# A fused adaLN block with attention and MLP: padding the last MLP tile, a new order of the tail, first loads on two rings, and reused buffers whose new writers are not ordered among themselves

## The chip, the cores and the metric

The kernel runs on one core of a Trainium2 chip. The metric is the device time of one execution, in microseconds (us), as the median of several. "PE" is the matmul engine and "PEld" its weight loads, "DVE" the vector engine, "ACT" the activation engine, "POOL" the general-purpose engine, and "SP" the engine that in this kernel does nothing but issue transfers. ACT and POOL issue transfers too. A "score" matmul multiplies queries by K, a "PV" matmul the result by V. hT is the normalised x of a chunk, transposed, from which the queries are made (the "first projection"). An issuing engine has a "ring", the queue that its transfers stand in.

## The reference, cut to what matters

```python
x = A_x                                    # 2048 x 640, bf16
sa, ca, ga, sb, cb, gb = split(silu(c) @ w_mod)        # 640 -> 6 x 640
h = layernorm(x) * (1 + ca) + sa
x = x + ga * attention(h, k_cache, v_cache, wq, wo)    # 32 heads of 128, 2048 keys
h = layernorm(x) * (1 + cb) + sb
x = x + gb * B(h)

def B(x):                                  # F = 1728 = 13 * 128 + 64
    h  = gelu(layernorm(x) @ w1)
    hs = concat(four column groups of h, shifted by 1, -1, 2, -2 rows) @ w2
    x1 = x + hs
    return x1 + gelu(layernorm(x1) @ w3) @ w4
```

F is not a multiple of 128: the last of the 14 tiles of W3's columns and W4's rows has 64.

## The kernel before

The kernel is written for a list scheduler. Every operation names its engine, what it reads and writes, and a priority; `Plan` puts the operations of each engine in one order and adds the semaphores. The queries are split in four chunks of 512. Attention is a long steady part; the MLP, the tail, comes at the end. Parts of the tail are named by letters: A is W1 of a chunk, B is W2 of 128 rows, C is W3 of a chunk, D is W4 of 128 rows, WO is the last output projection of attention, and I3 the layer norms of the last chunk. K0, V0, V1, V3 are the K and V of head 0, 1, 3; W_o and Wq are the weights of the output and the query projections; X1 is the x of chunk 1.

```python
class Plan:
    FIRST = {"PE": 3, "ACT": 10000, "DVE": 0, "POOL": 7, "SP": -5}   # where the branch to the fast program stands
    HINT  = {"PE": 0, "ACT": -30, "DVE": 0, "POOL": 0, "SP": -12}    # and its prefetch hint

    def op(self, eng, fn, dur, reads=(), writes=(), prio=0.0, ...):
        for t in reads:
            for d in t.writer: o.deps[d] = True
            t.readers.append(o)
        for t in writes:
            ...
            for d in t.writer:  o.deps.setdefault(d, False)   # a new writer waits for the last writer
            for d in t.readers: o.deps[d] = True              # and for the readers
            t.writer = [o]                                    # and is the writer that the next one waits for
            t.readers = []
# ... the start: K transposes, Wq, x and most V on SP; the gate weights and V0 on ACT
    dma("ACT", lambda e: e.dma_start(pre_ap, mod_src(2)), 800, (wm[1],), pre_t, -292)      # gate weights
    load_v(0, -290, "ACT", gate=(wm[1],))                                                  # V0
    load_wq(0, 1, HG, -295.985, gate=(wm[2],))                                             # Wq, heads 1 to 3, on SP
# ... two of the five slices of hT of chunk 0 are made by ACT, the others by DVE
            for k in (0, 2, 4, 1, 3):
                if k % 2:
                    P.op("ACT", lambda e, k=k: e.activation(hT_t[0][:, k, :], hslice(k, 0, 4), ACT.Identity, ...
# ... the transposes of the normalised chunk into a buffer that held other data (nT_old)
                dmaT(lambda e, i=i: e.dma_start_transpose(nT_ap[ch][:, :, i * 128:(i + 1) * 128], xn[i].ap), 160,
                     (xn[i],), (nT[ch][i],) + nT_old[ch](), prio)
# ... the tail
    TAIL = ("A0 B0 B1 A1 B2 B3 WO B4 B5 I3 A2 B6 C0 B7 D0 D1 D2 B8 D3 B9 C1 D4 A3 B10 B11 "
            "B12 D5 B13 D6 B14 D7 B15 C2 D8 D9 D10 D11 C3 D12 D13 D14 D15").split()
    WOD, CH, I3D = -100, -1000, -200
    def w4_tile(t, key):
        for hf in range(2):
            for f in range(NF):                    # NF = 14, FS = [128] * 13 + [64]
                fs = FS[f]
                P.op("PE", lambda e, ...: e.matmul(m[:, hf * 512:hf * 512 + HD], gT_ap[0:fs, f, i * 128:(i + 1) * 128],
                                                   w4_ap[f][0:fs, hf * HD:(hf + 1) * HD], start=(f == 0), stop=(f == NF - 1)), ...
```

## Time and profile before

| | us |
|---|---|
| time before, median of 3 | 1391.6 (1391.36 to 1391.62) |
| profiled span | 1391.3 |
| first score matmul | 18.11 |
| first W1 matmul (the tail begins) | 1207.44 |
| from there to the end | 183.9 (1391.3 - 1207.44) |

These are two lines of the page of the kernel before: PE's busy time with its share of the span, and the shares of the chain that ended last.

```profile
PE 1379.4 (99%) x13128; PEld 941.2 (68%) x13128; DVE 539.6 (39%) x1401; ACT 1101.5 (79%) x1143; POOL 100.9 (7%) x88
...
PE 97%; DVE 1%; DMA 1%; SPq 0%; issue 0%; ACT 0%
```

PE is busy all the time, and the chain is PE. So a change can pay only at PE: fewer or quicker matmuls, or fewer of its few waits.

The next lines are from PE's timeline before, in the tail. Columns: start, duration, engine, line of the program, operation, output from inputs, shapes, count, and in brackets the idle time before it and what ended it.

```profile
1258.56 4.28 PE L928 MATMUL f_M<-f_KV,f_OO 128*128 128x320 bf16 x28
1262.77 4.29 PE L928 MATMUL f_S<-f_KV,f_OO 128*128 128x320 bf16 x28
```

One W4 tile follows the other every 4.22 us, with 28 matmuls each. The timeline of PE's weight loader shows what is peculiar in each tile:

```profile
1260.42 1.85 PEld L928 LDWEIGHTS f_M<-f_KV,f_OO 64*128 64x128 bf16 x14 [0.26 <-issue]
1262.53 0.09 PEld L928 LDWEIGHTS f_M<-f_KV,f_OO 64*128 64x128 bf16 x1 [0.26 <-issue]
```

The loader stands still 0.26 us around each load of 64 rows (usually 0.04).

PE's timeline at the last output projection, before:

```profile
1225.74 0.71 PE L691 MATMUL f_S<-f_wo,f_OO 128*128 128x320 bf16 x4
1227.88 0.72 PE L691 MATMUL f_O<-f_wo,f_OO 128*128 128x320 bf16 x4 [1.43 <-DVE f_tmp L702]
...
1229.67 1.25 PE L691 MATMUL f_O<-f_wo,f_OO 128*128 128x320 bf16 x4 [0.54 <-DVE f_small L500]
1230.72 1.27 PE L691 MATMUL f_S<-f_wo,f_OO 128*128 128x320 bf16 x4
1231.78 2.14 PE L887 MATMUL f_M<-f_W,f_PQ 128*128 128x320 bf16 x10
```

There are two waits for DVE, 1.43 and 0.54 us, and then matmuls at half speed (1.25 us for the same group that took 0.72). The windows view gives a granted clock of 0.50 between 1230 and 1232 us.

PE's timeline at the start, before:

```profile
13.38 0.25 PE L448 MATMUL f_M<-f_s_bf,f_W 128*128 128x1 bf16 x4 [1.34 <-issue]
...
18.11 0.59 PE L734 MATMUL f_S<-f_PQ,f_KV 128*128 128x512 bf16 x2
...
49.17 0.61 PE L753 MATMUL f_O<-f_KV,f_PQ 128*128 128x129 bf16 x8 [1.94 <-DMA f_KV<-in_A_v_cache_dram]
```

A gap of 1.34 us with no releaser ("issue"), the first score matmul at 18.11, and a wait of 1.94 us for V3. PE's early branch itself is at 6.4 us (by the view of its line, L252).

### The profile page before, as it was taken

To read this page: it belongs to the slowest core of one execution; us is meant where nothing else is said; L and a number is where in the kernel's file an instruction comes from. 1 tells how busy PE (TensorE), PEld (TensorE's weight loads), DVE (VectorE), ACT (ScalarE), POOL (GpSimd) and SP (SyncE) were. 2 spreads that over 40 slices of the span, in tenths; PEclk is the share of its full clock that TensorE was granted. 3 is DMA by queue.
4 is the path that set the end of the run, shared out by engine and by line. 5 is a ranking of instruction groups with operands and counts; after the bars stand their busy time and mean duration, and the time that the engine had idled before them with its cause. 6 is when DMAs were issued, how large, how long until landed. Compare 5 with 4: busy or idle time off the path is not lost.

```text
span 1391.3 us, 29861 instructions
## 1 busy us (share of the span) xinstructions
PE 1379.4 (99%) x13128; PEld 941.2 (68%) x13128; DVE 539.6 (39%) x1401; ACT 1101.5 (79%) x1143; POOL 100.9 (7%) x88
## 2 busy tenths in 40 slices
PE   9999999999999999999999999999999999999999
PEld 6667767777777777777777776777776766645554
DVE  5453232333233322333233323332333245987553
ACT  5888888888888898888888888888888888732222
POOL 0000000000000000000000000000333248200000
PEclk9999999999999999999999999999999999999999
DMA  9651623161214221241205122612254102531210
GB/s 220 130 115 31 117 78 83 36 107 35 46 36 84 58 46 36 48 92 30 54 17 98 31 45 36 107 36 46 55 91 114 17 16 48 120 53 24 53 43 25
DMA packets 259179, 88.90 MB, mean 64 GB/s; under 512 B 236705, under 2 KB 257762, under 8 KB 259042
## 3 DMA queue, kind: packets, MB, share of 16 engines
q1 hardware_dynamic: 255762, 84.59, 30.7%
q10 hardware_dynamic: 3280, 2.33, 0.7%
q8 instruction: 105, 1.72, 0.5%
q14 instruction: 32, 0.26, 0.1%
HBM read 43.48 MB, written 2.62 MB: 33 GB/s over the span
## 4 chain that ended last, share of the span: by engine, by line
PE 97%; DVE 1%; DMA 1%; SPq 0%; issue 0%; ACT 0%
PE f_O L753 33%; PE f_S L734 31%; PE f_M L666 10%; PE f_M L691 10%; PE f_M L928 3%; PE f_S L914 2%; PE f_O L914 2%; PE f_S L928 2%; PE f_S L887 1%; PE f_S L864 1%; PE f_O L864 1%; PE f_M L887 1%; DMA f_W<-in_w_mod_dram 0%; DMA f_KV<-in_A_v_cache_dram 0%; SPq L573 0%; PE f_M L610 0%
## 5 line engine op out<-in xcount | busy, mean ns | idle before, releaser
L736 ACT ACTIVATE f_PQ<-f_S 128x1024 bf16<-128x1024 f32 x1024 | 1041.0, 1023 | 148.2 <-PE f_S L734 135.1
L753 PEld LDWEIGHTS f_O<-f_KV,f_PQ 128*128 128x128 bf16 x8192 | 589.4, 98 | 233.7 <-issue 2.4
L734 PE MATMUL f_S<-f_PQ,f_KV 128*128 128x512 bf16 x2048 | 726.9, 379 | 0.2 <-ACT f_PQ L736 0.2
L753 PE MATMUL f_O<-f_KV,f_PQ 128*128 128x129 bf16 x8192 | 713.0, 220 | 2.7 <-DMA f_KV<-in_A_v_cache_dram 1.9
L699 DVE TENSOR_TENSOR f_y<-f_M,f_y 128x320 f32<-128x320 f32 x192 | 94.3, 491 | 536.3 <-PE f_M L691 536.3
L691 PE MATMUL f_M<-f_wo,f_OO 128*128 128x320 bf16 x992 | 272.9, 299 | 0.0
L734 PEld LDWEIGHTS f_S<-f_PQ,f_KV 128*128 128x128 bf16 x2048 | 196.7, 97 | 30.5 <-ACT f_PQ L736 1.2
L666 PE MATMUL f_M<-f_hT,f_wq 128*128 128x512 bf16 x640 | 177.3, 381 | 1.1 <-DVE f_hT L568 0.6
L691 PEld LDWEIGHTS f_M<-f_wo,f_OO 128*128 128x128 bf16 x992 | 96.1, 98 | 28.5
L762 DVE TENSOR_TENSOR f_OO<-f_O,f_rl 128x256 bf16<-128x256 f32 x256 | 108.4, 423 | 8.1
L669 DVE CAST f_PQ<-f_M 128x512 bf16<-128x512 f32 x128 | 88.5, 691 | 56.9 <-PE f_M L666 56.8
L520 POOL TENSOR_TENSOR f_y<-f_y,f_mod 128x640 f32<-128x640 f32 x32 | 49.6, 1560 | 820.1 <-DVE f_y L699 819.9
L666 PEld LDWEIGHTS f_M<-f_hT,f_wq 128*128 128x128 bf16 x640 | 62.2, 98 | 65.9 <-DVE f_hT L575 1.5
L760 DVE RECIPROCAL f_rl<-f_O 128x2 f32<-128x2 f32 x256 | 43.4, 169 | 32.1 <-PE f_O L753 27.9
L928 PE MATMUL f_M<-f_KV,f_OO 128*128 128x320 bf16 (+1 forms) x308 | 47.1, 300 | 0.0
L917 ACT ACTIVATE f_OO<-f_O 128x512 bf16<-128x512 f32 (+1 forms) x28 | 16.6, 596 | 38.5 <-PE f_O L914 38.5
L526 ACT ACTIVATE f_xn<-f_y,f_small 128x640 bf16<-128x640 f32 x10 | 9.1, 915 | 41.6 <-DVE f_small L505 41.6
L928 PEld LDWEIGHTS f_M<-f_KV,f_OO 128*128 128x128 bf16 (+1 forms) x308 | 28.6, 97 | 18.7 <-issue 7.0
L697 DVE COPY f_y<-f_M 128x320 f32<-128x320 f32 x32 | 15.7, 490 | 63.5 <-PE f_M L691 63.5
L481 DVE BATCH_NORM_STATS2 f_small<-f_y 128x6 f32<-128x320 f32 x64 | 29.6, 480 | 2.0 <-POOL f_y L520 2.0
L917 ACT ACTIVATE f_OO<-f_S 128x512 bf16<-128x512 f32 (+1 forms) x28 | 16.7, 595 | 13.1 <-PE f_S L914 13.1
L942 DVE TENSOR_TENSOR f_y<-f_M,f_y 128x640 f32<-128x640 f32 x10 | 8.2, 825 | 43.2 <-PE f_M L928 43.2
(134 smaller groups left out, 513.9 us busy)
## 6 DMA issues: line engine op xcount, KB each, us to landing
f_KV<-in_A_v_cache_dram SPq DMA_DIRECT2D x31, 512.0 KB, 4.8
f_wo<-in_A_wo_dram SPq DMA_DIRECT2D x8, 640.0 KB, 4.4
f_xin<-in_A_x_dram SPq DMA_DIRECT2D x15, 320.0 KB, 4.6
f_wq<-in_A_wq_dram SPq DMA_DIRECT2D x7, 640.0 KB, 4.6
f_W<-in_w_mod_dram SPq DMA_DIRECT2D x3, 800.0 KB, 4.9
out_dram<-f_xin SPq DMA_DIRECT2D x15, 160.0 KB, 1.8
f_KV<-in_B_w_dram SPq DMA_DIRECT2D x5, 432.0 KB, 3.3
f_KV<-in_A_k_cache_dram SPq DMA_TRANSPOSE x128, 2.7
```

The source lines that it names most:

```text
L520: P.op(eng, lambda e: e.tensor_tensor(out=out, in0=a, in1=b, op=op), COST[eng][0], rd, wr, prio, lat=300 if eng == "POOL" else None)
L666: P.op("PE", lambda e, i=i, kk=kk: e.matmul(m.ap, wq_t[g % 2][:, kk, hh * 128:(hh + 1) * 128], hT_t[ch][:, kk, :], start=(i == 0), stop=(i ...
L669: P.op("DVE", lambda e: e.tensor_copy(q.ap, m.ap), 690, (m,), (q,), s * NP - 90)
L691: P.op("PE", lambda e, m=m, qt=qt, hf=hf, hh=hh: e.matmul(m[:, 0:HD], OT_ap[gs][:, qt, hh, :], wo_t[g % 2][:, hh, hf * HD:(hf + 1) * HD], ...
L699: P.op("DVE", lambda e, m=m, yt=yt: e.tensor_tensor(out=yt.ap, in0=m[:, 0:HD], in1=yt.ap, op=ALU.add), 490, (m, yt), (yt,), s * NP - 60)
L734: P.op("PE", lambda e, sp=sp, r=r, kt=kt: e.matmul(sp[:, r * QC:(r + 1) * QC], K_ap[b][:, kt * 128:(kt + 1) * 128], q.ap, start=True, stop ...
L736: x = P.op("ACT", lambda e, sp=sp, pt=pt: e.activation(pt.ap.rearrange("p k q -> p (k q)"), sp.ap, ACT.Exp, scale=SCALE), 1021, (sp,), (pt ...
L753: ins = e.matmul(o[bk][:, w * 129:w * 129 + 129], pt[:, r, qt * 128:(qt + 1) * 128], V_ap[b][:, u, 0:129], start=(u == 0 and w == 0), stop ...
L760: P.op("DVE", lambda e, ov=ov, i0=i0: e.reciprocal(rl_t[:, i0:i0 + 2].unsqueeze(2), ov[:, 0:258].rearrange("p (u d) -> p u d", u=2)[:, :, ...
L762: evac.append(P.op("DVE", lambda e, ov=ov, i0=i0, bk=bk: e.tensor_tensor(out=On_ap[gs][:, 2 * bk:2 * bk + 2, hh, :], in0=ov[:, 0:258].rear ...
L914: P.op("PE", lambda e, m=m, f=f, kk=kk, fs=fs: e.matmul(m[0:fs, :], w3_ap[:, kk, f * 128:f * 128 + fs], nT_ap[ch][:, kk, :], start=(kk == ...
L928: P.op("PE", lambda e, f=f, hf=hf, fs=fs: e.matmul(m[:, hf * 512:hf * 512 + HD], gT_ap[0:fs, f, i * 128:(i + 1) * 128], w4_ap[f][0:fs, hf ...
```

## The change

It has five parts.

1. **Padding.** The last tile of W3 and W4 gets 128 columns and rows, the added half set to zero, so that no matmul has another shape.
2. **Tail order.** The last output projection moves behind W1 of chunk 2, and the DVE work that empties its banks gets priority.
3. **Start.** The first loads are divided between SP and ACT. ACT now issues the gate weights, Wq of heads 1 to 3, X1, V0 and V1; X1 goes into a buffer that nothing uses yet at the start.
4. **Writers not ordered.** A new argument `over` makes a new writer of a reused buffer wait for the old readers and writers, but the new writers do not wait for one another.
5. **Branch.** The branch to the fast program moves to the end of the first block on PE, DVE and POOL, with its prefetch hints. The scheduler's cost constants are adjusted too.

The diff, cut to its core:

```diff
-    FIRST = {"PE": 3, "ACT": 10000, "DVE": 0, "POOL": 7, "SP": -5}
-    HINT = {"PE": 0, "ACT": -30, "DVE": 0, "POOL": 0, "SP": -12}
+    FIRST = {"PE": 100000, "ACT": 100000, "DVE": -6, "POOL": 100000, "SP": -5}
+    HINT = {"PE": -300, "ACT": -30, "DVE": -60, "POOL": -1, "SP": -12}
@@ Plan.op
+        for t in over:
+            for d in t.writer:
+                o.deps.setdefault(d, False)
+            for d in t.readers:
+                o.deps[d] = True
@@ start
+            dma("ACT", lambda e: e.dma_start(y_t[:, 4:8, :].bitcast(BF16)[:, :, 0:D], x2d[512:1024, :]...),
+                640, (), xs + held, -296.7, after=(wm_load[3], ln0[1]))
-    dma("ACT", lambda e: e.dma_start(pre_ap, mod_src(2)), 800, (wm[1],), pre_t, -292)
+    dma("ACT", lambda e: e.dma_start(pre_ap, mod_src(2)), 800, (wm[3],), pre_t, -297, after=(ln0[0],))
-    load_v(0, -290, "ACT", gate=(wm[1],))
+    load_v(0, -296.5, "ACT", after=(ln0[1],))
+        if h in (1, 2, 3):
+            load_k(h, (-294, -291, -289)[h - 1], (wm[2],), () if h < 3 else from_slot(12))
+            load_v(h, (-293, -290, -289.5)[h - 1], "ACT" if h == 1 else "SP", () if h == 1 else (wm[2],), after=(ln0[1],) if h == 1 else ())
+            return
-    load_wq(0, 1, HG, -295.985, gate=(wm[2],))
+    load_wq(0, 1, HG, -296.8, eng="ACT", after=(ln0[0],))
@@ tail
-    TAIL = ("A0 B0 B1 A1 B2 B3 WO B4 B5 I3 A2 B6 C0 B7 D0 D1 D2 B8 D3 B9 C1 D4 A3 B10 B11 "
-            "B12 D5 B13 D6 B14 D7 B15 C2 D8 D9 D10 D11 C3 D12 D13 D14 D15").split()
+    TAIL = ("A0 B0 B1 A1 B2 B3 B4 A2 WO I3 B5 B6 C0 B7 D0 D1 D2 D3 B8 C1 B9 B10 A3 D4 B11 "
+            "B12 D5 B13 D6 D7 B14 B15 C2 D8 D9 D10 D11 C3 D12 D13 D14 D15").split()
-    WOD, CH, I3D = -100, -1000, -200
+    WOD, CH, I3D = -1000, -1000, -150
-                     (xn[i],), (nT[ch][i],) + nT_old[ch](), prio)
+                     (xn[i],), (nT[ch][i],), prio, over=nT_old[ch]())
@@ the same over= for the loads of W3 and W4, gT and some memsets (cut)
+    P.op("POOL", lambda e: e.memset(w3_ap[:, :, FF:FP], 0.0), 300, (), (pad,), E + 12, over=kv(2, 3, 4))
+    P.op("DVE", lambda e: e.memset(w4_ap[NF - 1][FL:128, :], 0.0), 400, (), (pad2,), E + 12, slack=500.0, over=kv(4))
-                P.op("PE", lambda e, ...: e.matmul(m[0:fs, :], w3_ap[:, kk, f * 128:f * 128 + fs], nT_ap[ch][:, kk, :],
+                P.op("PE", lambda e, ...: e.matmul(m.ap, w3_ap[:, kk, f * 128:(f + 1) * 128], nT_ap[ch][:, kk, :],
-                P.op("PE", lambda e, ...: e.matmul(..., gT_ap[0:fs, f, i * 128:(i + 1) * 128], w4_ap[f][0:fs, hf * HD:(hf + 1) * HD],
+                P.op("PE", lambda e, ...: e.matmul(..., gT_ap[:, f, i * 128:(i + 1) * 128], w4_ap[f][:, hf * HD:(hf + 1) * HD],
```

## The prediction

> **What bounds it.** The page gives PE 99% busy, the chain of waits is 97% PE, and the PE waits sum to about 10 us. Only PE time lost between matmuls, the start, and those few waits can pay.
>
> **1. Padding the last MLP tile.** Timeline of PE: a W4 tile is 28 matmuls of 320 columns and takes 4.22 us (4.12 when W2 follows, whose 10 matmuls then take 1.47 instead of 1.36). At the W2 pitch, 0.136 us, 28 would take 3.81. Around each 64-row weight load PE's loader sits idle 0.26 us for "issue", usually about 0.04. So each change between 64-row and 128-row matmuls costs about 0.11 us, four per tile. In W3 the 64-column group takes 1.20 instead of 1.08 and its successor about 0.11 more. The Trainium skill, "TensorEngine Tiling (Array Packing)", Key Properties, says that changing the tiling mode drains the engine; the trace agrees. Padded, count and streamed columns are equal and the changes vanish: 16 x 0.41 + 4 x 0.23 = -7.5 us, all on the critical path.
>
> **2. New order of the tail.** At 1225.7 to 1229.7 the last output projection waits 1.43 + 0.54 us for DVE (f_tmp evictions queued behind layer norms); then the granted clock falls to 0.50, and 4+4+10 matmuls take 1.06, 1.06 and 1.93 us instead of 0.54, 0.54 and 1.36: 1.6 us more. The change gives these evictions priority and moves them behind W1 of chunk 2. I expect -3 us.
>
> **3. Start.** The first score matmul begins at 18.1 us. A 1.34 us "issue" gap at 12.0, inside one group of matmuls, follows PE's early branch (instruction fetch, I think; the branch now stands at the end). After it the clock drops to about 0.8 and the first projection takes 2.34 instead of 1.08 us. At 47.2 PE waits 1.94 us for V of head 3, now loaded earlier. Possible gain 4 to 5 us. Against it: on the ACT ring 800 KB of gate weights, 480 KB of Wq and 640 KB of x now stand before V of head 0. The DMA share is full from 5 to 24 us at 210 to 390 GB/s; V0 landed at 20.0 and was needed at 21.8. By bytes I estimate that it now lands near 22 to 24, so PE may wait 2 to 4 us. Net -2 us (+2 to -5).
>
> **4. Writers not ordered among themselves.** This removes DMA-after-DMA waits that do not appear among PE's waits: 0.
>
> Steady attention (60 to 1195 us) should take the same time.
>
> Sum: -7.5 - 3 - 2 = -12.5 from 1391.6: **1379 us**, range 1373 to 1387. Faster by over 2% (below 1363.8) 2%, within 2% 97.5%, slower 0.5%.
>
> **What would show it.** Right: W4 tiles 3.8 us and W3 groups all 1.08; no 0.26 us loader gaps; output projection groups 0.54 each without a clock dip; first score matmul at 15.5 to 17; no V wait at 47; 60 to 1195 unchanged within 0.5 us. Wrong: W4 tiles still above 4 us; a PE wait over 3 us for V of head 0 or 1; a new DVE wait as large in the tail.
>
> **What would make the total wrong.** Late V0 with a cold clock after it (+4); DVE backlog moving to the next W2 or W3 (+3); a branch at the end of DVE or PE that costs a fetch in the output chain (+1); a start shorter by the full 5 us (-3).

## More of the kernel before

ACT's timeline at the start, before ("ACTq" is ACT issuing a transfer; the second line is V0):

```profile
7.18 0.39 ACTq L618 DMA_DIRECT2D f_KV<-in_w_mod_dram  x1
7.61 0.54 ACTq L588 DMA_DIRECT2D f_KV<-in_A_v_cache_dram  x1
...
14.25 0.78 ACT L564 ACTIVATE f_hT<-f_O,f_small 128x512 bf16<-128x512 bf16 x1 [3.02 <-PE f_M L559]
```

V0 is the last thing that ACT issues; its own part of hT begins at 14.25.

## The result, and the profile after

The kernel after takes 1387.29 us (median of 4, 1386.33 to 1387.92); the kernel before took 1391.48 (median of 4; three of them are those of the table above). A ratio here is the mean time of one kernel's fast runs over the mean of the other's fast runs of the same rounds, so it is not quite the ratio of the medians. It is 0.9973, with a 95% interval of 0.9956 to 0.999: by the limit of 2% the two are the same, and the gain is some 4 us instead of the predicted 12.5. The time lies just above the predicted range. All outputs are right.

Where it went can be read from one cut through the two traces, at the first W1 matmul:

| us | before | after | difference | predicted |
|---|---|---|---|---|
| first score matmul | 18.11 | 23.29 | +5.2 | 15.5 to 17 |
| first W1 matmul | 1207.44 | 1213.06 | +5.6 | -2 |
| from there to the end | 183.9 | 173.2 | -10.6 | -10.5 |
| profiled span | 1391.3 | 1386.3 | -5.0 | -12.5 |

The tail gained what was predicted, -10.6 against -10.5, but the close match is in part luck: the trace of the kernel before has 1.6 us of half clock that not every execution has (see "Padding alone"), and by the timing of the version with the old start the gain is nearer 9.5 us. The start lost over half of it. PE's timeline in the tail, after:

```profile
1236.49 0.71 PE L712 MATMUL f_S<-f_wo,f_OO 128*128 128x320 bf16 x4
1237.03 0.71 PE L712 MATMUL f_O<-f_wo,f_OO 128*128 128x320 bf16 x4
...
1260.26 3.97 PE L951 MATMUL f_M<-f_KV,f_OO 128*128 128x320 bf16 x28
1264.07 3.97 PE L951 MATMUL f_S<-f_KV,f_OO 128*128 128x320 bf16 x28
```

The output projection's groups come every 0.54 us without a wait, and a W4 tile takes 3.80 us instead of 4.22. Now the start, in ACT's timeline after:

```profile
8.32 0.54 ACTq L608 DMA_DIRECT2D f_wq<-in_A_wq_dram  x1
...
10.15 0.38 ACTq L552 DMA_DIRECT2D f_y<-in_A_x_dram  x1
10.57 9.59 ACTq L605 DMA_DIRECT2D f_KV<-in_A_v_cache_dram  x2
20.20 0.78 ACT L581 ACTIVATE f_hT<-f_O,f_small 128x512 bf16<-128x512 bf16 x1 [9.85 <-issue]
```

Issuing V0 and V1 takes 9.59 us (0.56 for V0, 8.99 for V1, by the view of that line's instructions). Until 20.16 ACT can do nothing else, and its two slices of hT, begun at 14.25 in the kernel before, begin at 20.20. The brackets say "issue": ACT waited for no semaphore, it was issuing. PE's timeline after shows who pays:

```profile
21.04 1.46 PE L687 MATMUL f_M<-f_hT,f_wq 128*128 128x512 bf16 x3 [6.61 <-ACT f_hT L581]
23.29 1.03 PE L755 MATMUL f_S<-f_PQ,f_KV 128*128 128x512 bf16 x2 [0.79 <-DVE f_PQ L690]
```

After the wait the matmuls run at half speed. In the windows view of after (columns: window, its length, busy time and count of PE, PEld, DVE, ACT and POOL, then the granted PE clock; the last two, the DMA share and GB/s, are not used here):

```profile
13.00:14.00 1.00, 0.39 (x1) 0.10 (x1) 1.00 (x3) 0.00 (x0) 0.00 (x0) 1.00 0.55 119
14.00:15.00 1.00, 0.39 (x1) 0.10 (x1) 0.43 (x1) 0.00 (x0) 0.00 (x0) 0.69 1.12 287
...
16.00:20.00 4.00, 0.00 (x0) 0.00 (x0) 0.00 (x0) 0.00 (x0) 0.00 (x0) 0.50 1.20 224
20.00:24.00 4.00, 2.17 (x5) 0.52 (x6) 0.69 (x1) 1.45 (x2) 0.00 (x0) 0.50 1.35 220
24.00:28.00 4.00, 4.00 (x14) 1.96 (x13) 0.61 (x2) 2.05 (x2) 0.10 (x1) 0.50 1.35 228
28.00:32.00 4.00, 4.00 (x37) 2.53 (x36) 3.18 (x9) 3.04 (x4) 0.03 (x1) 0.99 1.52 152
```

All compute engines stand idle from 16 to 20 us, and the clock is 0.50 until 28. The Trainium skill, "TensorE: Matmul & The Clock Gate", Part 1, says that the clock is halved after an idle window of about 3.4 us and comes back after as long a busy one. The return agrees: PE works without a wait from 23.29, and the clock is full again at about 28. The fall does not: it comes between 14 and 15 us, when the wait of 6.61 us has only begun (at 14.4) and PE's longest wait since 2 us was 0.68. The kernel before shows the same fall there (0.74 from 14 to 15 us) and is back at 1.00 by 18. So the long wait did not bring the clock down here; the clock stayed down until 28 instead of 18.

The Trainium skill, "Perfetto Trace Analysis", section "DMA Instruction — HWDGE", says that the profiled time of an issue includes waiting for the descriptor generator and generating, that the sequencer is free only after it, and that there is a buffer which can fill. So a long issue is a held engine, which is what ACT's timeline shows: 8.99 us against 0.56.

From 60 to 1195 us PE is busy for 1134.54 us in both kernels, at a clock of 1.00: no change, as predicted.

### The profile page after: what moved, and what is told of

Read it like the earlier page. It is cut to its first block, busy times and chain, and to the rows that moved or that the text cites. A ratio compares the mean times of both kernels' runs of the same rounds, so it can differ in the third digit from the quotient of the medians.

```text
span 1386.3 us, 29857 instructions
## 1 busy us (share of the span) xinstructions
PE 1371.0 (99%) x13128; PEld 944.9 (68%) x13128; DVE 540.3 (39%) x1402; ACT 1101.7 (79%) x1143; POOL 101.9 (7%) x89
## 3 DMA queue, kind: packets, MB, share of 16 engines
q10 hardware_dynamic: 6528, 4.00, 1.3%
## 4 chain that ended last, share of the span: by engine, by line
PE 97%; DVE 2%; ACTq 1%; ACT 0%; issue 0%; POOL 0%; POOLq 0%
PE f_O L774 33%; PE f_S L755 32%; PE f_M L687 10%; PE f_M L712 10%; PE f_S L951 2%; PE f_M L951 2%; PE f_S L938 2%; PE f_O L938 2%; PE f_S L889 1%; PE f_S L912 1%; PE f_M L912 1%; ACTq L605 1%; PE f_O L889 1%; DVE f_small L489 0%; PE f_M L627 0%; PE f_S L431 0%
## 5 line engine op out<-in xcount | busy, mean ns | idle before, releaser
L941 ACT ACTIVATE f_OO<-f_O 128x512 bf16<-128x512 f32 x28 | 16.7, 596 | 26.9 <-PE f_O L938 26.8
L941 ACT ACTIVATE f_OO<-f_S 128x512 bf16<-128x512 f32 x28 | 16.7, 596 | 24.9 <-PE f_S L938 24.9
L489 DVE BATCH_NORM_STATS2 f_small<-f_y 128x6 f32<-128x320 f32 (+1 forms) x72 | 33.0, 480 | 2.0 <-POOL f_y L528 2.0
L951 PE MATMUL f_M<-f_KV,f_OO 128*128 128x320 bf16 x224 | 31.7, 299 | 0.0
L951 PE MATMUL f_S<-f_KV,f_OO 128*128 128x320 bf16 x224 | 31.7, 299 | 0.0
L951 PEld LDWEIGHTS f_M<-f_KV,f_OO 128*128 128x128 bf16 x224 | 21.9, 98 | 8.9
```

The lines of the kernel that those rows point to most:

```text
L951: P.op("PE", lambda e, f=f, hf=hf: e.matmul(m[:, hf * 512:hf * 512 + HD], gT_ap[:, f, i * 128:(i + 1) * 128], w4_ap[f][:, hf * HD:(hf + 1) ...
```

## The experiments

My theory: the loss is ACT's compute standing behind a held issue. Rivals: V0's data is late (my own risk in the prediction); the start is bound by the bytes that must land and no order helps; or one of the other parts costs something. A second question is which of the parts the tail's gain belongs to.

### V1 issued by SP

```diff
-  load_v(h, ..., "ACT" if h == 1 else "SP", ...)
+  load_v(h, ..., "SP", (wm[2],))
```

> The changed kernel with one load moved: V of head 1 is issued by SP again and not by ACT. Theory H (held issuer): in the changed kernel ACT is held 9.0 us in the issue of V1 (11.17 to 20.16 us), and the two hT activations that PE needs stand behind it. Then ACT is free at about 11.2 us, the hT activations run at about 13.4, the first score matmul begins at 15.5 to 17.5 us and the total falls by 5 to 8 us against the changed kernel, to about 1380. Rival D (bytes): the data ring is simply full, and the loads that the start needs (Wq, V0, gate weights) come as late as they do anyway. Then PE waits for a DMA instead and the total falls by less than 2 us.

Measured: 1383.76 us (5 runs), ratio to before 0.9942 (0.9929 to 0.9955). ACT's issue of V0, and PE:

```profile
10.49 0.98 ACTq L605 DMA_DIRECT2D f_KV<-in_A_v_cache_dram  x1
```

```profile
16.25 0.61 PE L755 MATMUL f_S<-f_PQ,f_KV 128*128 128x512 bf16 x2 [0.79 <-DVE f_PQ L690]
23.88 0.61 PE L774 MATMUL f_O<-f_KV,f_PQ 128*128 128x129 bf16 x8 [3.29 <-DVE f_small L504]
```

The hold is gone, hT is made at 13.35 and the first score matmul comes at 16.25, as the theory said. The total falls by about 4 us by the ratios, short of the 5 to 8 that I expected, because some of it comes back at once: PE waits 3.29 us in front of the first PV matmul. The profile names a small DVE operation there, but V0 was issued at 10.49 and landed 13.3 us later, at 23.8, just when PE went on. So the risk of my prediction, a late V0, is real too; in the kernel after it was hidden behind the larger wait.

### Padding alone

```diff
 (the kernel before)
+    FP = NF * 128          # and the matmuls, memsets and offsets of part 1
```

> The kernel before with the padding alone. Theory: W4 tiles take 3.80 us instead of 4.22 and all W3 groups 1.08, the loader gaps of 0.26 us vanish, and the total falls by 7.5 us (7 to 8). A rival, that the extra rows cost as much as the changes of shape saved or that DVE then cannot keep up with the shorter W4 tiles, gives less than 4 us.

Measured: 1384.06 us (5 runs), ratio 0.995 (0.9937 to 0.9963). That is 0.5% of 1391.5, or 7.0 us, where 7.5 was predicted. Padding alone comes out faster than the whole change, though the two intervals just touch. In its trace the tail takes 174.7 us, 9.1 less than before, which is more than the padding can give. The rest is here, in PE's timeline:

```profile
1228.99 0.72 PE L691 MATMUL f_O<-f_wo,f_OO 128*128 128x320 bf16 x4 [0.54 <-DVE f_small L500]
1229.55 0.71 PE L691 MATMUL f_S<-f_wo,f_OO 128*128 128x320 bf16 x4
```

The two waits are there, to the hundredth of a us, but no half clock follows (0.72 instead of 1.25). So the 1.6 us of slow matmuls that I read from the trace of before do not come with every execution. The record agrees: of the eleven executions of the kernel before in these rounds, three have a mean clock of 1.000 and four of 0.997. In this run the clock did not fall at the start either (1.00 from 12 to 18 us).

### Tail order alone

```diff
 (the kernel before)
-    TAIL = ("A0 B0 B1 A1 B2 B3 WO B4 B5 I3 A2 B6 ...   WOD, I3D = -100, -200
+    TAIL = ("A0 B0 B1 A1 B2 B3 B4 A2 WO I3 B5 B6 ...   WOD, I3D = -1000, -150
```

> The kernel before with the new order of the tail and its priorities alone. Theory: the 1.43 and 0.54 us waits at the last output projection and the half clock after them (1.6 us more) vanish, the total falls by 3 us (2 to 4). Rival: DVE is the limit there and the wait moves to another group, so that the total falls by less than 1 us.

Measured: 1398.53 us (6 runs), ratio 1.0051 (1.0039 to 1.0063): 7 us slower than before, which neither the theory nor the rival had foreseen. PE's timeline has a new wait, and SP's shows why:

```profile
1234.06 2.32 PE L864 MATMUL f_O<-f_wq,f_sbc 128*128 128x512 bf16 x5 [7.76 <-DMA f_wq<-f_xn]
```

```profile
1218.87 6.86 SPq L811 DMA_TRANSPOSE f_wq<-f_xn  x3
1228.03 2.52 SPq L902 DMA_TRANSPOSE f_wq<-f_xn  x2
1230.60 1.28 SPq L811 DMA_TRANSPOSE f_wq<-f_xn  x1
```

W1 of chunk 2, now earlier, waits for the four transposes of that chunk (L811). They write four parts of one reused buffer, and each counts as a writer of the whole old buffer, so each waits for the one before; the scheduler then puts two transposes of other work (L902) before the fourth. In SP's timeline of the kernel after, the same four go back to back, and no PE wait is left:

```profile
1223.84 5.17 SPq L832 DMA_TRANSPOSE f_wq<-f_xn  x4
```

### The transposes ordered again, in the kernel after

```diff
-  (xn[i],), (nT[ch][i],), prio, over=nT_old[ch]())
+  (xn[i],), (nT[ch][i],) + nT_old[ch](), prio)
```

> The kernel after, with the four transposes of the normalised chunk ordered among themselves again (only this use of the new argument undone). Theory (the new tail order pays only because these transposes may now be issued back to back): the chunk-2 transposes are chained again as in the run with the tail order alone, PE waits 6 to 8 us in front of the first W1 matmuls of chunk 2 with the transposes' DMA named as releaser, a half-rate clock follows, and the time is 7 to 11 us above the kernel after, so 1394 to 1398 us, slower than the kernel before. Rival (the wait in that run came from the missing padding or from the old head): no such wait, within 2 us of the kernel after.

Measured: 1396.77 us (5 runs), ratio to before 1.0046 (1.0032 to 1.0059). In PE's timeline the wait is there:

```profile
1239.00 1.91 PE L889 MATMUL f_O<-f_wq,f_sbc 128*128 128x512 bf16 x4 [8.14 <-DMA f_wq<-f_xn]
```

This one line of the change is worth some 10 us with the new order in place (1.0046 less 0.9973, of 1391). I had valued it at 0.

### Tail order with the new argument, without padding and with the old start

```diff
 (the kernel before) + the tail order + over=
```

> The kernel before with the new tail order and the new argument for reused buffers, and nothing else (no padding, old start). Theory (these two are a pair: the order alone lost 7 us because the transposes of chunk 2 were chained): no wait over 1 us before W1 of chunk 2, no wait for DVE in the output projection, 2 to 4 us below the kernel before: 1387.5 to 1389.5 us, ratio 0.997 to 0.9985. Rival (the loss of the order alone came from the unpadded tiles' timing): a wait of 5 us or more for the transposes and 1393 us or more.

Measured: 1388.44 us (5 runs), ratio 0.9988 (0.9974 to 1.0002): about 1.7 us, at the edge of what can be told from nothing. The traces say that the mechanism is right: no wait for DVE in the output projection and none for the transposes, 180.0 us from W1 to the end against 183.9 before (of which 1.6 are the half clock that is not always there). So order and argument are a pair: the first without the second costs 7 us, both together gain about 2 us, which the timing alone does not tell from nothing.

This run shows one more thing, in PE's timeline at the start:

```profile
15.45 0.25 PE L453 MATMUL f_M<-f_s_bf,f_W 128*128 128x1 bf16 x4 [3.37 <-issue]
...
20.08 0.61 PE L739 MATMUL f_S<-f_PQ,f_KV 128*128 128x512 bf16 x2
```

The gap that the early branch leaves was 3.37 us here instead of 1.34, and the first score matmul came 2.0 us later than in the kernel before. Yet the wait of 1.94 us for V3 was gone, and W1 began at 1206.76, not later than the 1207.44 of before. PE came later, and V3 was not later: by SP's timelines it was issued at 43.50 us here and at 44.35 in the kernel before. So in these two traces the gap and the wait for V3 do not add up: the later PE comes, the less of the wait is left. That it is so in every execution is not shown.

### Branch alone

```diff
 (the kernel before)
-    FIRST = {"PE": 3, ...       HINT = {"PE": 0, ...
+    FIRST = {"PE": 100000, ...  HINT = {"PE": -300, ...
```

> The kernel before with the branch to the second block moved to the end of PE, POOL and DVE, alone. Theory: the 1.34 us issue gap of PE at 12.0 us was the fetch after the branch, it vanishes, the first score matmul begins 1 to 2.5 us earlier and the total falls by 1 to 2.5 us. Rival: the gap is a fetch that comes with the place in the stream, not with the branch; it stays somewhere in the first 20 us and the total stays within 0.7 us.

Measured: 1391.96 us (6 runs), ratio 1.0002 (0.999 to 1.0014): nothing. The gap is gone and the first score matmul comes at 15.10 instead of 18.11; so the early branch did make the gap. The Trainium skill, "Runtime: NRT & Kernel Launch", section "Instruction fetch mechanics", says that branching breaks the sequential prefetch; this pair of traces fits (1.34 us with, none without), but the gap comes over 5 us after the branch and not at it, so that it is instruction fetch is not shown. But in PE's timeline the wait for V3 has grown:

```profile
47.43 0.62 PE L753 MATMUL f_O<-f_KV,f_PQ 128*128 128x129 bf16 x8 [2.47 <-DMA f_KV<-in_A_v_cache_dram]
```

It ends at 47.43 instead of 49.17, so 1.7 of the 3.0 us were left by then (V3's own issue had moved too, from 44.35 to 42.10 by SP's timelines); the timing over six runs shows none of it, though its interval leaves room for a gain of 1.4 us.

### What holds ACT: three orders on its ring

```diff
 first:  X1 issued by SP, V1 stays on ACT
 second: V1 by SP, the first part of W_o (640 KB in 512 rows) in its place on ACT
 third:  V1 by SP, V0 ahead of X1 on ACT
```

> The kernel after, with x of chunk 1 issued by SP instead of ACT; both V loads stay on ACT. Theory (ACT is held in V1's issue until what is ahead of it on ACT's own ring has drained): with only the q weights ahead of V0 and V1, ACT is free at about 16 to 18 us instead of 20.2, and the first score matmul comes at 19 to 21 us instead of 23.3. Rival (the hold is a fixed cost of a load of 2048 rows, or is set by the other engine's loads): V1's issue still takes 9 us or more and ACT is free at 20 us or later.

Measured: ACT's issue of V0 and V1 took 6.57 us, until 16.78; first score matmul at 19.91; 1383.84 us in one run. In ACT's timeline:

```profile
10.21 6.57 ACTq L605 DMA_DIRECT2D f_KV<-in_A_v_cache_dram  x2
```

This fits the theory (16 to 18 and 19 to 21 us), not the rival.

> The kernel after, with V1 issued by SP and a load of 640 KB in 512 long rows (the first part of W_o, needed only much later) in V1's place on ACT; V1 is 512 KB in 2048 rows of 256 bytes. Theory by rows (what holds the issuer is the number of small rows queued on its ring): the hold is at most 3.5 us and ACT is free by 14 us. Rival by bytes (the issuer is held until the bytes ahead have moved): held until about 20 us, as with V1.

Measured: ACT was held in the issue of W_o until 19.17, though it has few rows; 1387.0 us in one run. ACT's timeline:

```profile
10.90 8.27 ACTq L613 DMA_DIRECT2D f_wo<-in_A_wo_dram  x1
```

My theory by rows, in the form that it had here (the held load itself matters), fell. The number fits the rival by bytes, but the next two runs speak against that.

> The kernel after, with V1 issued by SP and V0 put ahead of x of chunk 1 on ACT's ring. Theory (after V1 has gone, what is left of the lost time at the start is V0 landing last on a ring that x of chunk 1 shares): V0 lands by about 18 us instead of 23.8, the 3.29 us wait in front of the first PV matmul is under 1 us, the first score matmul stays at 16 to 17 us, and the time is 3 to 6 us below the version with V1 on SP alone, 1378 to 1381 us. Rival (the bytes of both rings land together whatever their order, or x of chunk 1 becomes the new limit): a wait of 2 us or more appears elsewhere in the first 40 us, and the time is within 2 us of that version.

Measured: 1384.23 us (5 runs), ratio 0.9952 (0.9939 to 0.9966), no better than V1 on SP alone. Now X1 is held, behind V0. ACT's timeline:

```profile
10.22 0.42 ACTq L605 DMA_DIRECT2D f_KV<-in_A_v_cache_dram  x1
10.68 8.02 ACTq L552 DMA_DIRECT2D f_y<-in_A_x_dram  x1
```

Both expectations missed this: the wait came back on ACT itself, 4.29 us of PE waiting for hT, first score at 21.83. It also answers the rival by bytes: X1 is held with 1792 KB ahead of it on the ring (800 gate weights, 480 Wq, 512 V0), while V0 with 1920 KB ahead of it (800, 480, 640) was issued in 0.98 us in the run with V1 on SP.

### Five loads of long rows on ACT, no V

```diff
 (the kernel after, with V0 and V1 issued by SP)
+  ACT: gate weights, Wq, X1, W_o part 1, W_o part 2      # 2560 KB ahead of the fifth
```

> The kernel after with five loads of long rows on ACT and no V load: gate weights (800 KB), q weights (480), x of chunk 1 (640), and the first two parts of W_o (640 each) where V0 and V1 stood; V0 and V1 are issued by SP. At the fifth issue 2560 KB are ahead of it on ACT's ring, more than the 2432 KB ahead of V1 in the kernel after. Theory (the issue is held by a load of 2048 short rows waiting ahead of it): no issue on ACT takes more than 1.5 us, and ACT is free by 12 us. Rival (what counts is the number of loads or of bytes ahead): the fifth issue is held 6 us or more, until about 18 to 20 us.

Measured: the two W_o issues took 1.49 us each and ACT was free at 13.47 (I had said 12). In ACT's timeline:

```profile
10.46 3.01 ACTq L613 DMA_DIRECT2D f_wo<-in_A_wo_dram  x2
```

More bytes ahead, as many loads, and no hold of 6 us or more: neither the bytes nor the number of loads sets it. (The run itself is slow, 1389.24 us, since K transposes now stand behind V0 on SP and PE waits 7.9 us for K.)

Put together, with landing times from each run's view of transfers:

| run | load in front of V0, landed | load behind V0, its issue ended |
|---|---|---|
| after | X1, 20.3 | V1, 20.16 |
| X1 on SP | Wq, 17.0 | V1, 16.78 |
| W_o on ACT | X1, 19.4 | W_o, 19.17 |
| V0 first | Wq, 19.1 | X1, 18.70 |
| V1 on SP | X1, 18.6 | nothing behind V0: no hold |
| long rows | no V on ACT | longest issue 1.49 us |

In all four held cases the load behind V0 is held until 0.1 to 0.4 us before the load in front of V0 has landed. V0 itself lets the engine go within 1 us. Another rival, that ACT waits for SP's K transposes, does not fit: with V1 on SP these are issued from 3.57 to 20.11 us too, and ACT is not held. What sets V0 apart from the others is its many short rows: taking V1 off ACT's ring took 6528 - 4464 = 2064 packets off it, putting W_o in its place brought 528 (512 KB and 640 KB). A buffer for descriptors (the pieces that an issued load is split into) that V0 cannot enter until what is ahead of it has drained would explain it, but no run measured the buffer, so that stays an interpretation; the rule in the table is measured, on ACT's ring and in these four runs. It does not carry over as it stands. In the run of long rows, SP has a K transpose behind V0:

```profile
9.52 7.19 SPq L600 DMA_TRANSPOSE f_KV<-in_A_k_cache_dram  x1
```

This is a long hold behind a V load again, but it ends at 16.71, while the transfer in front of V0 had landed at 11.1.

### V0 and V1 issued by POOL

```diff
-    load_v(0, -296.5, "ACT", ...);  load_v(1, -293, "ACT", ...)
+    load_v(0, -296.5, "POOL", (wm[2],));  load_v(1, -293, "POOL", (wm[2],))
```

> The kernel after with V0 and V1 issued by POOL, which has nothing urgent behind them, instead of ACT; ACT keeps the gate weights, the q weights and x of chunk 1. Theory (the loss is ACT's compute standing behind a held issue, so any issuer without work behind it cures it): no hold on ACT, hT activations at 13.4 us, first score matmul at 16 to 17 us; V0 no longer waits behind the q weights and x of chunk 1 on one ring, so it lands by 20 us, the wait in front of the first PV matmul is under 2 us, and the time is 1379 to 1383 us, at or below the version with the old start, 1381.9. Rival (the start is bound by the bytes that must land in it, whichever ring carries them): the wait only moves to another load, V0 to 23 us or K or V of a later head, and the time is 1383 to 1386 us.

Measured: 1383.71 us (5 runs), ratio 0.9946 (0.9933 to 0.996). hT at 13.52 and first score at 16.42, with no wait for V0: the theory of the held issuer holds again. POOL itself was not held: V1, directly behind V0, took 1.16 us to issue, and on its queue the two loads count only 288 packets. But in PE's timeline another load is late, as the rival said:

```profile
22.47 2.21 PE L687 MATMUL f_M<-f_hT,f_wq 128*128 128x512 bf16 x5 [3.23 <-DMA f_wq<-in_A_wq_dram]
```

Wq of heads 1 to 3 now lands 13.7 us after its issue, against 8.6 in the kernel after. The time falls in the range of the rival.

### The old start with everything else

```diff
 (the kernel before) + padding + tail order + over=
```

> The kernel before with the padding, the new tail order and the new argument for reused buffers: the kernel after with its whole start undone (loads, rings and branch position as in the kernel before). Theory (the start alone lost about 5.6 us, and the other three parts are worth what the tail shows, 10.5 us): the first score matmul at 18.1 us as in the kernel before, no wait over 1 us before W1 of chunk 2 in the tail, 1380 to 1382 us, ratio 0.992 to 0.993. Rival (the parts of the tail are worth less without the new start, because the buffers' loads come at other times): 1384 us or more.

Measured: 1381.9 us (5 runs), ratio 0.9932 (0.9918 to 0.9945). This is the kernel after without its start, its branch and the adjusted cost constants (the tail and the steady part show no effect of these: 173.3 us to the end against 173.2), and it is better than the kernel after (0.9956 to 0.999; each against its own runs of the kernel before), and so beats both kernels. First score at 17.03, W1 at 1206.55, 173.3 us to the end. In PE's timeline the only wait of over 1 us for a transfer is the old one for V3:

```profile
47.79 0.62 PE L758 MATMUL f_O<-f_KV,f_PQ 128*128 128x129 bf16 x8 [1.89 <-DMA f_KV<-in_A_v_cache_dram]
```

### The old loads with the branch: a slip, then the corrected run

```diff
 (the version with the old start) + branch +
 the slip:      K and V of heads 2 and 3 with the priorities of the kernel after
 the corrected: only V3 directly behind V2, ahead of K3
```

> As the run with the old start, plus the branch moved to the end of the streams with its prefetch hints, plus V of heads 2 and 3 loaded as early as in the kernel after; ACT issues only the gate weights and V0, as in the kernel before. Theory (the branch move saves about 3 us up to the first score matmul, and the run with the branch alone lost them only to V of head 3, 2.5 us at 45 to 47 us): the first score matmul at about 15.1 us, V0 in time or at most 2 us late, no wait for V of head 3, and 2 to 4 us below the version with the old start: 1377 to 1379 us. Rival (the start is bound by the bytes that must land, and each wait taken away comes back at the next load): within 1 us of the version with the old start.

Measured: 1387.64 us (5 runs), ratio 0.9972 (0.9958 to 0.9986), so nearly 6 us slower than the version with the old start. My edit gave V2 a priority (-290) ahead of V1's (-289). PE's timeline:

```profile
36.40 1.05 PE L762 MATMUL f_O<-f_KV,f_PQ 128*128 128x129 bf16 x8 [5.50 <-DMA f_KV<-in_A_v_cache_dram]
```

That wait is of my own making, and the run tells nothing about the theory.

> The version with the old start (padding, new tail order and the new argument, start as in the kernel before), plus the branch moved to the end with its prefetch hints, plus V of head 3 alone issued directly after V of head 2 and before K of head 3. This repeats the intent of the run with the old loads and the branch without its slip: there V of head 2 had been given a priority ahead of V of head 1. Theory (the branch move is worth about 2 us up to the first score matmul, and V of head 3 about 2 us at 45 to 48 us, and neither comes back): first score matmul at 15 to 16 us, no wait over 1 us for V or K in the first 60 us, 2 to 4 us below the version with the old start, so 1377.5 to 1380 us, ratio 0.990 to 0.992. Rival (the start is bound by what must land, so the waits come back at other loads): waits of 2 us or more for K, V or hT before 60 us and 1381 to 1383 us.

Measured: 1381.89 us (5 runs), ratio 0.9938 (0.9925 to 0.9952), like the version with the old start. First score at 15.82 and no wait for V; but in PE's timeline:

```profile
19.38 1.25 PE L671 MATMUL f_M<-f_hT,f_wq 128*128 128x512 bf16 x5 [1.22 <-DMA f_wq<-in_A_wq_dram]
46.65 0.39 PE L671 MATMUL f_M<-f_hT,f_wq 128*128 128x512 bf16 x1 [2.58 <-DVE f_hT L580]
```

The waits moved to Wq and to hT of chunk 1, whose transposes stand behind V3 and K3 on SP. The rival was right: what is gained at the first score is paid back by another load within 50 us.

### All runs in one table

Between kernels with the old start and the old branch the first W1 matmul comes at 1206.6 to 1208.1, so about 1.5 us of the third column is scatter of single executions. Ratios are to the kernel before of the same rounds; runs of one look have none.

| run | first score | first W1 | from W1 to end | ratio |
|---|---|---|---|---|
| before | 18.11 | 1207.44 | 183.9 | 1 |
| after | 23.29 | 1213.06 | 173.2 | 0.9973 |
| padding alone | 17.32 | 1206.76 | 174.7 | 0.995 |
| tail order alone | 16.77 | 1208.09 | 190.6 | 1.0051 |
| tail order and argument | 20.08 | 1206.76 | 180.0 | 0.9988 |
| branch alone | 15.10 | 1205.68 | 183.2 | 1.0002 |
| after, transposes ordered | 23.32 | 1212.87 | 182.0 | 1.0046 |
| after, V1 on SP | 16.25 | 1208.80 | 172.7 | 0.9942 |
| after, X1 on SP (one look) | 19.91 | 1209.89 | 172.6 | |
| after, W_o on ACT (one look) | 22.30 | 1213.00 | 172.6 | |
| after, V0 first | 21.83 | 1212.15 | 172.6 | 0.9952 |
| after, long rows on ACT (one look) | 16.21 | 1214.51 | 173.3 | |
| after, V0 and V1 on POOL | 16.42 | 1209.71 | 172.6 | 0.9946 |
| old start, all else | 17.03 | 1206.55 | 173.3 | 0.9932 |
| old start, branch, the slip | 15.88 | 1213.46 | 173.2 | 0.9972 |
| old start, branch, V3 | 15.82 | 1209.17 | 172.4 | 0.9938 |

## Why the prediction was right or wrong

The total was wrong: 1379 predicted, 1387.29 measured, above the range of 1373 to 1387. The class (within 2%) was right.

**Step 1, padding, "-7.5 us, all on the critical path": right.** A W4 tile takes 3.80 us (predicted 3.81), and padding alone gives 7.0 us.

**Step 2, the tail, "I expect -3 us": about half right for the pair, wrong as a part of its own.** Alone the order costs 7 us. With the new argument it gives 1.7 us by the timing (not clear of zero) and 3.9 us in one trace, 1.6 of which are the half clock. I had counted the half clock after the waits (1.6 us) as a steady cost; the run with padding alone has the same waits and no half clock.

**Step 3, the start, "Net -2 us (+2 to -5)": this is the step that failed.** It came out at +5.6, outside its own range. The sentence at fault is "By bytes I estimate that it now lands near 22 to 24, so PE may wait 2 to 4 us". Its estimate was nearly right (V0 landed at 24.4 in the kernel after). What failed is the path: it took the data of V0 for the only way in which the loads given to ACT could hold PE up. I asked when the data would land and how long PE would wait for it, and not what happens to the engine that issues. ACT was held 8.99 us in the issue of V1, with two slices of hT behind it in its own order, and PE waited 6.61 us for these. Moving V1 alone to SP brings the first score matmul from 23.29 to 16.25 and about 4 us of the time back (0.9973 to 0.9942). The late V0 that I had warned of then appears (landing at 23.8, wait 3.29 us), so that mechanism was right and second in line.

The other half of step 3 was wrong too: "Possible gain 4 to 5 us" added the branch's gap, the half clock after it and the wait for V3. The branch alone gains nothing that the timing shows (1.0002), in one trace a gap of 3.37 us instead of 1.34 loses nothing by the first W1 matmul, and with padding alone a gap of 1.27 us has no half clock after it. PE only reaches the next late load sooner or later. Every division of the loads that did not hold ACT still left PE waiting for one of them in the first 50 us: V0 (3.29 us), Wq (3.23 and 1.22), hT of chunk 1 (2.58), V3 (1.89) or K (7.9). (hT of chunk 1 comes out of DMA transposes, so it counts as a load here.) I did not find a start that beats the old one, and whether there is one stays open.

**Step 4, writers not ordered, "0": wrong.** I looked for the waits that it removes among PE's waits of the kernel before, and there were none. They would have come with the new order of step 2: ordering the transposes again in the kernel after costs 10 us. Two parts of one change must be valued together where one takes away the slack that the other needs.

**The steady part: right.** From 60 to 1195 us nothing changed.

## What to carry to other kernels

Before giving a compute engine another load to issue, look at what stands behind the issue in that engine's own order: here a load behind one with 2064 packets held ACT for 8.99 us, until the loads ahead of that one had all but landed, and 1.5 us of activations came 6 us later than before. A gap in front of a late load may cost nothing; test whether lengthening it changes the end. And value an ordering constraint against the new schedule, not the old one, whose slack may hide it.

## What the Trainium skill lacked or had wrong

- "DMA: Bandwidth & Descriptors", section "Issuing engines are not separate DMA queues", says that issuing on several engines saves only the sequencer's time to initiate, "which is usually small relative to the DMA itself". Here spreading cost time: ACT's issue of V1 took 8.99 us of the 16.2 us to its landing, and PE lost 6.61 us to the activations behind it. The page has no warning of that for engines that also compute.
- "Perfetto Trace Analysis", section "DMA Instruction — HWDGE", draws a descriptor buffer that fills, but gives no size and no rule for when an issuer is held. On ACT's ring four runs show that the load behind one of 2064 packets (512 KB) is held until 0.1 to 0.4 us before the load in front of that one lands, and one run that loads of some 528 packets are not held, with 2560 KB ahead (1.49 us). On SP a transpose behind such a load was held too (7.19 us), but until 5.6 us after the landing in front.
- "TensorE: Matmul & The Clock Gate", section "HAM oscillation — how this bites in real kernels", gives as its rule no idle gaps over about 3.4 us. In the kernel before, waits of 1.43 and 0.54 us were followed by a clock of 0.50; with padding alone the same two waits were not. In the kernel after, the clock fell at about 14.4 us, when no wait since 2 us had been over 0.68. That page's Part 1 says that the window runs freely and that results vary with its phase, which fits both outcomes, and its next section names frequent short idles as a cause; what it lacks is how short and how many (two, of 1.97 us together, cost 1.6 us here).
- No page says that the gap an early branch leaves can come well after it (over 5 us, in the kernel before) or how much it varies: in five traces with the branch at the same place it was 0.61 to 3.37 us, always in front of the same group of matmuls.
